# One routing of nine row tiles, late scatters and a second load queue in an attention and mixture-of-experts kernel

## The chip, the cores and the metric

The kernel runs on one core of a Trainium2 chip. The core has a matrix engine (PE, with PEld for its weight loads), a vector engine (DVE), an activation engine (ACT), a general engine (POOL, which also issues the indirect transfers) and a queue engine (SP, which issues most of the other transfers). The engines run their own instruction streams in order and wait for each other by semaphores. The metric is the device time of one execution in microseconds (us), the median of several runs.

## The reference

Three stages follow each other on 2304 tokens of width 512. The first is attention with 8 heads in which a row keeps only its 32 largest scores. The second routes each token to the one expert of eight with the largest gate logit. The third does the same with other weights, but only for tokens with a positive skip score, and adds its result to the token.

```python
kth = np.partition(scores, -32, axis=-1)[..., -32:-31]
attn = softmax(np.where(scores >= kth, scores, -1e9)) @ v
x = attn_out.transpose(0, 2, 1, 3).reshape(2304, 512)
e = argmax(x @ w_gate); g = softmax(x @ w_gate)[e]
x[mask_e] = g * (relu(x[mask_e] @ w1[e]) @ w2[e])                # layer one
x[mask_e] = x[mask_e] + g * (relu(x[mask_e] @ w1[e]) @ w2[e])    # layer two, tokens with x @ w_skip > 0
```

## The kernel before

**Attention.** The 4 batches are taken two at a time (a half), the 8 heads two at a time (a unit), so there are 8 units of 9 row tiles, 72 groups g in all. Units 0 to 3 are the first half, 4 to 7 the second. Each group passes through some twenty small stages, one letter each in `attention`: scores on PE (A), their copy to SBUF on ACT (AE), the search for the 32 largest on DVE (A1, lines 190 to 209), a check of the count with a sign pass on ACT and a product y on POOL (Bs, line 228) and its maximum on DVE (C, line 235), the masked exponentials (Dr, Dz, Dx, Dm), transposes and the product with v on PE (E, F), and the normalized row on DVE (Fin, line 346). For some (group, head) pairs POOL subtracts the mask (Dr, line 274); for the others DVE multiplies by it (Dm, line 291). The order is written out by hand: lines 389 to 421 give each stage of each group a step `tau` and a rank `z` within the step, and the instructions go out step by step. In the steady part a step does the work of one group for every stage, and the pattern of mask variants repeats every six groups.

**Routing.** When the last unit of a half has finished a row tile, the tile (x, three row tiles in one buffer, and parts, the shares of the gate logits) is routed: `Ga` adds seven small DVE instructions to the list `small`, `Gr` issues an exponential and small matrix products that count places, and adds eight more DVE instructions and the scatters. A1 takes one entry of `small` after each of its 14 MAX8 instructions; after step 73 the list is emptied at the end of each step. Before, `gate_tiles` routes three row tiles at a time (lines 637 to 676). In the first half the three sets are pulled apart by six steps each (line 402), and their nine scatters are spread over later steps by `LATE` (lines 410 and 411, `Sc`). A scatter (line 605) is an indirect transfer that POOL issues: 128 rows of 2056 bytes to their places in `ev.rows[0]` in HBM. The last three row tiles of the second half are routed one by one (`gate_rows`). The buffers x are five, so the third one of the second half takes the place of the first one of the first half.

**Weights.** `Moe.fetch(k)` loads chunk k (512 KB, eight chunks for each expert: four of w1, four of w2) on SP into one of eight raw buffers; `Moe.split(k)` makes a high part (ACT, line 765) and a low part (POOL or DVE, line 767) of it and then fetches the chunk that follows in the buffer. During attention three raw buffers exist; chunks 0 to 3 are split in steps 1, 2, 3 and 5, and chunks 4, 5 and 11 are loaded ahead.

**The layers.** `Moe.layer` loads the first expert's four blocks of rows (`load`, line 774, on SP), keeps PE warm with 26 transposes (line 691), loads the counts, and fetches chunks 6 to 10. `Moe.expert` transposes the blocks (`xT`, line 802), then runs eight first products (`mm1`, line 818) with the splits between them, and the second products (`mm2`, line 842). Blocks 2 and 3 of an expert stand under a condition on the count of its rows. `Moe.open` zeroes a part of XT on ACT (line 732).

Of the kernel before, what the change touches and what calls it, by code (L numbers as in the profile page):

```python
# [42 lines left out]
LATE = ((2, 4, 6), (2, 5, 8), (2, 5, 8))  # L43
# [67 lines left out]
def spare_places(tc, ev, s):  # L111


    ev.counts = s[:, 0, 0, 288:342].rearrange("p (a b) -> p a b", b=9)
    ev.onehot = [s[:, 0, 1, 288 + 54 * i:342 + 54 * i].rearrange("p (a b) -> p a b", b=9) for i in range(2)]
    ev.gates = [[s[:, 1, h, 288 + 48 * i + 24 * w:312 + 48 * i + 24 * w].rearrange("p (t e) -> p t e", e=8)
                 for h in range(2) for w in range(2)] + [s[:, 0, 0, 344 + 8 * i:352 + 8 * i]] for i in range(2)]
    ev.logits = [s[:, 1, 0, 384 + 8 * i:392 + 8 * i] for i in range(3)]
    ev.placed = [s[:, 1, 1, 384 + 8 * i:392 + 8 * i] for i in range(3)]
    tc.nc.vector.tensor_copy(ev.counts, ev.iosel[:, None, :].to_broadcast([128, 6, 9]))  # L120
# [23 lines left out]
def attention(tc, ev, q, k, v, during):  # L144
    nc = tc.nc
# [188 lines left out]
    def Fin(g):  # L334
        u, j = divmod(g, 9)
        e = G[g]
        kb, i, n = where[g]
        bp, hp = divmod(u, HP)
        if hp == 0 and j % 3 == 0:
            x[bp, j // 3] = ev.xp.tile([128, 3, HP * 128 + 2], F32, name="x", bufs=5)  # L340
            parts[bp, j // 3] = ev.xp.tile([128, 3, HP * 2, 8], F32, name="parts", bufs=5)
            nc.gpsimd.tensor_copy(x[bp, j // 3][:, :, HP * 128 + 1], ev.tok[:, bp * 9 + j:bp * 9 + j + 3])
        rows, shares = x[bp, j // 3][:, j % 3], parts[bp, j // 3][:, j % 3]
        for out, at, w in ((rows[:, hp * 128:hp * 128 + 128].rearrange("p (a b) -> p a b", a=2), 0, 64),
                           (shares[:, hp * 2:hp * 2 + 2], 128, 8)):
            nc.vector.tensor_tensor(out, e["po"][:, at:at + 2 * w].rearrange("p (a b) -> p a b", a=2),  # L346
                                    BT[kb]["ri"][:, 2 * i:2 * i + 2, None].to_broadcast([128, 2, w]), op=OP.mult)
        del G[g]

    def gated(g):  # L350

        u, j = divmod(g, 9)
        bp, hp = divmod(u, HP)
        n = 1 if g >= NG - 3 else 3 if j % 3 == 2 else 0
        return (bp, j // 3, j % 3 + 1 - n, n) if hp == HP - 1 and n else None

    def Ga(g):
        at = gated(g)
        if at:
            bp, k, t, n = at  # L360
            rt = bp * 9 + k * 3 + t
            if n > 1:
                a, rest, c = gate_tiles(tc, ev, sb, x[bp, k], parts[bp, k], rt, ev.gates[k % 2])
# [26 lines left out]
    for g in range(NG):  # L390
# [3 lines left out]
        for z, (nm, fn, at) in enumerate((  # L394
# [242 lines left out]
def gate_tiles(tc, ev, sb, x, parts, rt, places):  # L637

    nc = tc.nc
    v, n = nc.vector, x.shape[1]  # L640
    Dm = x.shape[2] - 2
    lg, order, row, mine, sums = places
    f = sb.tile([128, 3, 8], F32, name="tf", bufs=2)
    ed = sb.tile([128, 3, 8], F32, name="ted", bufs=2)
    ob = ev.onehots[rt // 3 % 2]
    ix = sb.tile([128, 3], I32, name="tix", bufs=2)
# [3 lines left out]
    def rest():  # L650
        nc.scalar.activation(ed, ed, AF.Exp)
        p = ev.ps.tile([128, 4, 8], F32, name="m", bufs=ev.mb)
        nc.tensor.matmul(p[:, :n + 1], ev.tri, ob[:, :n + 1], start=True, stop=False)
# [4 lines left out]
    def logits():  # L658
        v.tensor_reduce(out=lg, in_=parts.rearrange("p t h e -> p t e h"), op=OP.add, axis=AX.X)

    return [logits,
# [48 lines left out]
class Moe:  # L710
# [4 lines left out]
    def __init__(self, tc, ev, pool, weights):  # L715
        self.tc, self.ev, self.ws = tc, ev, weights
        self.W1 = [pool.tile([128, 2, 1024], F32R, name="w1_%d" % i) for i in range(4)]
        self.RAW = [pool.tile([128, 1024], F32, name="raw%d" % i) for i in range(3)]

    def open(self, sb, psum, posts):  # L720
# [10 lines left out]
        for c in range(4):  # L731
            self.tc.nc.scalar.activation(self.XT[:, c, :, 256:], self.ev.zrow[:, :512].rearrange("p (a n) -> p a n", a=2),
                                         AF.Copy)
        self.W1 += [sb.tile([128, 2, 1024], F32R, name="w1_%d" % (4 + i)) for i in range(NW - 4)]
        self.RAW += [sb.tile([128, 1024], F32, name="raw%d" % (3 + i)) for i in range(NR - 3)]
# [5 lines left out]
    def raw(self, k):  # L741

        return self.RAW[k % 3 if k < 4 else (k - 3) % NR]

    def fetch(self, k):
# [5 lines left out]
        raw, c = self.raw(k), k % 8  # L751
        if c < 4:
            self.tc.nc.sync.dma_start(raw, w1[e, c * 128:(c + 1) * 128, :])
        else:
            self.tc.nc.sync.dma_start(raw.rearrange("p (a d) -> p a d", a=2),
                                      w2[e, (c - 4) * 256:(c - 3) * 256, :].rearrange("(a p) d -> p a d", p=128))

    def split(self, k, vector=()):
# [9 lines left out]
        self.fetch(k + (3 if k < 3 else NR))  # L768

    def load(self, g, j):  # L770
# [3 lines left out]
        self.tc.nc.sync.dma_start(self.XG[g % 2][j], rows[r0:r0 + 128])  # L774
# [79 lines left out]
    def expert(self, g):  # L854
# [6 lines left out]
        self.optional(g, lambda j: self.xT(g, j))  # L861
        if e:
# [3 lines left out]
        if nxt:  # L866
            for j in range(BLOCKS[layer]):
                self.load(g + 1, j)
        k = 8 * g + 8
        for f in range(8):  # L870
# [4 lines left out]
            if f in FN:  # L875
                self.split(k, post.lo)
                k += 1
            self.tick()
            if f == 4 and nxt:
                self.counts(e + 1)  # L880
        if g == 15:
            self.tc.nc.gpsimd.drain()  # L882
        steps = {}
# [21 lines left out]
    def layer(self, layer, ns):  # L905
# [3 lines left out]
        for j in range(BLOCKS[layer]):  # L909
            self.load(g0, j)  # L910
# [5 lines left out]
        if layer == 0:  # L916
            for k in range(6, 3 + NR):
                self.fetch(k)
# [157 lines left out]
def attention_moe_kernel(ctx: ExitStack, tc, q, k, v, wg1, w11, w12, wskip, wg2, w21, w22, out):  # L1076
# [30 lines left out]
    ev.onehots = [consts.tile([128, 4, 8], BF, name="oh%d" % i) for i in range(2)]  # L1107
# [98 lines left out]
```

## Time and profile before

| | before |
|---|---|
| median of 3 runs | 1040.43 us (1039.23 to 1041.92) |
| the profiled execution, device time | 1037.0 us |
| its span in the trace | 1035.2 us |
| busy in the span: PE, DVE, ACT, POOL | 891.0, 747.0, 675.5, 627.7 us |

Attention fills roughly the first 493 us of the span, layer one the time up to about 800 us, layer two the rest. Busy shares over the whole span are therefore means over stages that have different limits. A row of a timeline gives start, duration, engine, line, operation, the tile written and the tiles read, and in brackets how long the engine had stood idle and what released it. DVE instructions are pipelined, so a printed duration reaches some 0.06 to 0.1 us into the next one; where work is priced below, starts are compared with starts where that can be done.

### The profile page before, as it was taken

The page shows a single profiled execution, that of the slowest core. Times are in us where ns is not written, and L with a number is a line of the kernel's source. Part 1 is how long each engine was busy: PE and PEld are TensorE (multiplying, and loading weights), DVE is VectorE, ACT ScalarE, POOL GpSimd, SP SyncE. Part 2 cuts the span into 40 slices and gives each one's busy share as a digit, 9 for nine tenths or more (in the row PEclk, how much of TensorE's full clock was granted, in tenths as well). Part 3 has the DMA queues.
Part 4 walks back from the last instruction along what each step waited for, and adds up shares of the span by engine and source line. Part 5 has one row for each costly group of instructions (what it writes and reads, how often), then busy time and mean ns, then how long its engine had stood idle before and what let it go on. Part 6 is the DMA issues. An engine that isn't in the chain of part 4 may idle for free. (4 is left out here: it accounts for less than half of the span.)

```text
span 1035.2 us, 20565 instructions
## 1 busy us (share of the span) xinstructions
PE 891.0 (86%) x6305; PEld 708.6 (68%) x6305; DVE 747.0 (72%) x3438; ACT 675.5 (65%) x1344; POOL 627.7 (61%) x446
## 2 busy tenths in 40 slices
PE   7578778877878778777899989998999899999997
PEld 5355545555555555555788879877887888888886
DVE  6999999999999999998328545356553356654362
ACT  6699999999989988975436434445553355543352
POOL 5888887887877978953225334344533366654454
PEclk9699999999989989989799999999999799999999
DMA  7897010100202000001635544466534367664540
GB/s 261 263 306 225 20 47 24 47 25 1 80 21 80 12 11 21 12 1 73 235 112 171 181 136 149 135 197 205 183 93 140 124 205 218 219 209 156 183 128 27
DMA packets 55032, 127.71 MB, mean 123 GB/s; under 512 B 8105, under 2 KB 8105, under 8 KB 54864
## 3 DMA queue, kind: packets, MB, share of 16 engines
q1 hardware_dynamic: 48464, 112.89, 34.8%
q0 software_dynamic: 6400, 12.65, 3.3%
q8 instruction: 97, 1.59, 0.6%
q14 instruction: 71, 0.58, 0.2%
HBM read 96.04 MB, written 37.86 MB: 129 GB/s over the span
## 5 line engine op out<-in xcount | busy, mean ns | idle before, releaser
L767 POOL TENSOR_TENSOR w<-raw,w 128x1024 fp32r<-128x1024 f32 x74 | 178.8, 2429 | 202.2 <-ACT w L765 151.9
L228 POOL TENSOR_TENSOR y<-s,sg 128x576 f32<-128x576 f32 x144 | 209.1, 1473 | 48.0 <-ACT sg L225 42.6
L842 PE MATMUL y<-w,h 128*128 128x512 f32 x936 | 227.8, 395 | 7.3 <-DVEq L791 3.3
L818 PE MATMUL hp<-xT,w 128*128 128x192 f32 (+4 forms) x1536 | 218.6, 300 | 5.3 <-DVE h L833 3.0
L818 PEld LDWEIGHTS hp<-xT,w 128*128 128x128 f32 x1536 | 208.5, 194 | 9.8 <-DVE h L833 5.6
L842 PEld LDWEIGHTS y<-w,h 128*128 128x128 f32 x936 | 171.4, 188 | 48.8 <-issue 8.4
L197 DVE MAX8 ca<-s 128x8 f32<-128x82 f32 (+1 forms) x1008 | 156.3, 228 | 6.2 <-ACT s L186 6.2
L274 POOL TENSOR_TENSOR r<-s,r 128x576 f32<-128x576 f32 x96 | 135.9, 1429 | 17.1 <-DVE r L270 11.9
L833 DVE SCALAR_TENSOR_TENSOR h<-hp,h 128x512 fp32r<-128x512 f32 (+1 forms) x128 | 77.9, 620 | 82.7 <-ACT h L832 82.6
L832 ACT ACTIVATE h<-hp 128x512 fp32r<-128x512 f32 (+1 forms) x128 | 69.8, 545 | 101.5 <-PE hp L818 94.2
L765 ACT ACTIVATE w<-raw 128x1024 fp32r<-128x1024 f32 x128 | 133.4, 1054 | 0.5 <-ACTq L791 0.5
L310 PE MATMUL m<-ident,p 128*128 128x128 f32 x576 | 96.5, 296 | 33.5 <-DVE parts L346 20.9
L225 ACT ACTIVATE sg<-s,tm 128x576 f32<-128x576 f32 x144 | 111.9, 796 | 7.1 <-POOL tm L216 6.8
L310 PEld LDWEIGHTS m<-ident,p 128*128 128x128 f32 x576 | 66.5, 148 | 72.3 <-ACT p L282 20.7
L767 DVE TENSOR_TENSOR w<-raw,w 128x1024 fp32r<-128x1024 f32 x54 | 94.7, 1753 | 21.5 <-ACTq L791 12.8
L99 PE MATMUL s<-kT,qT 64*128 64x288 f32 x512 | 86.3, 457 | 21.2 <-DVE kths L241 7.6
L235 DVE MAX8 my<-y 128x8 f32<-128x576 f32 x144 | 101.9, 746 | 1.6 <-POOL y L228 1.5
L186 ACT ACTIVATE s<-s 128x1152 f32<-128x1152 f32 (+1 forms) x73 | 81.6, 1119 | 20.5 <-PE s L99 10.6
L138 PE MATMUL m<-pT,v 128*64 128x128 f32 (+1 forms) x1280 | 90.2, 289 | 2.7 <-ACT pT L316 2.6
L316 ACT ACTIVATE pT<-m 128x512 f32<-128x512 f32 x144 | 80.9, 608 | 8.4 <-PE m L310 8.2
L138 PEld LDWEIGHTS m<-pT,v 128*64 128x64 f32 x1280 | 71.4, 151 | 15.4 <-ACT pT L316 5.0
L282 ACT ACTIVATE p<-r,neg 128x576 f32<-128x576 f32 x96 | 75.3, 785 | 6.4 <-POOL r L274 5.9
(160 smaller groups left out, 1225.6 us busy)
## 6 DMA issues: line engine op xcount, KB each, us to landing
raw<-in_moe_w_dram SPq DMA_DIRECT2D x128, 512.0 KB, 4.3
x<-zrow SPq DMA_DIRECT2D x16, 1028.0 KB, 19.0
xg<-x SPq DMA_DIRECT2D x56, 257.0 KB, 3.6
v<-in_v_dram SPq DMA_DIRECT2D x8, 576.0 KB, 3.7
kT<-in_k_dram SPq DMA_DIRECT2D x7, 576.0 KB, 3.8
qT<-in_q_dram SPq DMA_DIRECT2D x7, 576.0 KB, 4.9
out_dram<-yo,ix POOLq DMA_INDIRECT x40, 4.9
kT<-in_k_dram SPq DMA_DIRECT2D x2, 288.0 KB, 3.8
```

The costliest lines, as they stand in the source:

```text
L99: nc.tensor.matmul(p[:, c, :288], d["qT"][h, b, t * 128:t * 128 + 128], d["kT"][h, b, cs], start=True, stop=True)
L138: nc.tensor.matmul(po[i * 64:i * 64 + 64, cs], d["vt"][:, b, i, c] if c < 4 else d["v8"][i * 64:i * 64 + 64, b], pts[i][:, c, cs] if c < 4 ...
L197: nc.vector.max(out=ca[:, c], in_=e["s"][hh][:, cut[c]:cut[c + 1]])
L225: nc.scalar.activation(sg, e["s"][hh], AF.Sign, bias=bt["tm"][:, w:w + 1], scale=-ONE_BELOW, accum_out=bt["ac"][:, w:w + 1])
L228: nc.gpsimd.tensor_mul(y, e["s"][hh], sg)
L235: nc.vector.max(out=bt["my"][:, 2 * i + hh, 8:], in_=e["y"][hh])
L274: nc.gpsimd.tensor_tensor(r, e["s"][hh], r, op=OP.subtract)
L310: nc.tensor.transpose(pp[:, c], e["p"][:, hh, c * 128:c * 128 + 128], ident)
L765: nc.scalar.activation(t[:, 0], raw, AF.Copy)
L767: eng.tensor_tensor(t[:, 1], raw, t[:, 0].bitcast(F32), op=OP.subtract)
L818: nc.tensor.matmul(p[:, :W], self.w1(g, c)[:, a, fs], x[:, c, b, :W], start=(i == 0), stop=(i == 11))
L842: nc.tensor.matmul(p, self.HT[f][:, a, js], self.W2[f // 2][:, b, f % 2 * 512:f % 2 * 512 + 512], start=(f + a + b == 0), stop=(f == 7 and ...
```

## The change

- The first half's nine row tiles are routed in one set (`gate_tiles` with nine tiles, own tiles `whole`, `ev.half`, a ten-wide one-hot tile) after group 35, in steps 47 and 48; `Gr` follows `Ga` after one step instead of two, for the second half's first set too.
- Its nine scatters go out three each in steps 75, 76 and 77; the reciprocals are kept in a tile w, and one POOL copy for each three tiles puts them into the rows before the scatters.
- There are six x buffers. Two of them serve as raw buffers 1 and 2 in the first steps, and only one raw buffer is left of its own. Of the later chunks only chunk 4 is loaded during attention.
- In layer one, blocks 1 and 3 of the first expert are loaded on ACT's queue, and the zeroing of XT stands after these loads. Chunks 5 to 11 and the four blocks of the second expert are loaded on ACT's queue too: three right after the transposes of the first expert, and one in each of its eight first-product steps.

```diff
-LATE = ((2, 4, 6), (2, 5, 8), (2, 5, 8))
+LATE = (27, 27, 27, 28, 28, 28, 29, 29, 29)
+XB = 6
...
-            x[bp, j // 3] = ev.xp.tile([128, 3, HP * 128 + 2], F32, name="x", bufs=5)
+            x[bp, j // 3] = ev.xp.tile([128, 3, HP * 128 + 2], F32, name="x", bufs=XB)
...
-        n = 1 if g >= NG - 3 else 3 if j % 3 == 2 else 0
+        n = 1 if g >= NG - 3 else 9 * (j == 8) if bp == 0 else 3 * (j % 3 == 2)
...
-                ("Dx", Dx, m - 1), ("F", F, m + 2), ("Ga", Ga, m + 4), ("Gr", Gr, m + 6))):
+                ("Dx", Dx, m - 1), ("F", F, m + 2), ("Ga", Ga, m + 4), ("Gr", Gr, m + 5))):
...
-            if nm[0] == "G" and gated(g) and g < NG // 2:
-                at += g % 9 // 3 * 6
...
-                for t in range(3):
-                    plan.setdefault(at + LATE[g % 9 // 3][t], []).append((z, g, Sc))
+                for t in LATE:
+                    plan.setdefault(at + t, []).append((z, g, Sc))
...
-def gate_tiles(tc, ev, sb, x, parts, rt, places):
+def gate_tiles(tc, ev, sb, xs, parts, ob, places):
...
+    def send(t):
+        if n > 3 and t % 3 == 0:
+            nc.gpsimd.tensor_copy(xs[t // 3][:, :, Dm], w[:, t:t + 3])
+        scatter(tc, ev, ev.rows[0], ix[:, t:t + 1], xs[t // 3][:, t % 3], ev.group)
...
-            lambda: v.reciprocal(x[:, :, Dm], sums[:, n:2 * n]),
-            lambda: v.tensor_copy(ix[:, :n], sums[:, :n])] + [
-            lambda t=t: scatter(tc, ev, ev.rows[0], ix[:, t:t + 1], x[:, t], ev.group) for t in range(n)]
+            lambda: v.reciprocal(xs[0][:, :, Dm] if n == 3 else w, sums[:, n:2 * n]),
+            lambda: v.tensor_copy(ix, sums[:, :n])] + [lambda t=t: send(t) for t in range(n)]
...
-        return self.RAW[k % 3 if k < 4 else (k - 3) % NR]
+        return self.RAW[k % 3 if k < 4 else (k - 4) % NR]
...
-        self.fetch(k + (3 if k < 3 else NR))
+        if k < 1 or k > 2:
+            self.fetch(k + (1 if k == 3 else NR if k else 3))
...
+        first = []
+        if g == 0:
+            first = [lambda k=k: self.fetch(k, self.tc.nc.scalar) for k in range(5, 4 + NR)]
+            first += [lambda j=j: self.load(1, j, self.tc.nc.scalar) for j in range(BLOCKS[0])]
+            for i in range(3):
+                first.pop(0)()
...
-        if nxt:
+        if nxt and g:
             for j in range(BLOCKS[layer]):
                 self.load(g + 1, j)
...
+            if first:
+                first.pop(0)()
             self.tick()
...
         for j in range(BLOCKS[layer]):
-            self.load(g0, j)
+            self.load(g0, j, nc.scalar if layer == 0 and j % 2 else nc.sync)
+        if layer == 0:
+            for c in range(4):
+                nc.scalar.activation(self.XT[:, c, :, 256:], ...)
...
-        if layer == 0:
-            for k in range(6, 3 + NR):
-                self.fetch(k)
...
+        rows = [sb.tile([128, 3, Dm + 2], F32, name="x", bufs=XB) for i in range(2)]
+        moe.RAW += [t.rearrange("p t d -> p (t d)")[:, :1024] for t in rows]
```

## Rows read from the trace of the kernel before

**Rows 1.** Page: busy tenths of PE in 40 slices.
```profile
PE   7578778877878778777899989998999899999997
```
**Rows 2.** Stretches: start:end and length, DVE busy (instructions), clock, DMA share, GB/s.
```profile
195.47:208.49 13.02, 12.95 (x79) 1.00 0.26 93
195.47:231.95 36.48, 36.27 (x221) 1.00 0.15 51
231.95:270.00 38.05, 37.84 (x237) 0.91 0.10 33
270.00:312.23 42.23, 42.02 (x228) 0.92 0.10 34
312.23:350.17 37.94, 37.73 (x229) 0.91 0.16 55
350.17:390.15 39.98, 39.77 (x236) 0.91 0.04 15
390.15:428.85 38.70, 38.49 (x221) 0.91 0.04 15
428.85:443.90 15.05, 14.98 (x79) 1.00 0.05 19
```
**Rows 3.** Timeline of DVE, last steps of attention: line 291, POOL idle, first and last.
```profile
468.21 0.80 DVE L291 SCALAR_TENSOR_TENSOR p<-s,kths,e 128x576 f32<-128x576 f32 x1
...
477.04 0.81 DVE L291 SCALAR_TENSOR_TENSOR p<-s,kths,e 128x576 f32<-128x576 f32 x1
```
**Rows 4.** Timelines of POOL and then DVE around a scatter of the first half.
```profile
271.15 1.22 POOL L605 DMA_INDIRECT x<-x,tix  x1 [0.17 <-issue]
272.62 1.42 POOL L274 TENSOR_TENSOR r<-s,r 128x576 f32<-128x576 f32 x1
...
272.66 2.00 DVE L291 SCALAR_TENSOR_TENSOR p<-s,kths,e 128x576 f32<-128x576 f32 x1
```
**Rows 5.** Tile parts: the routing's first reduction, ns min/median/max, of three tiles and one.
```profile
L659 DVE TENSOR_REDUCE s<-parts x5: 486/494/517, 242.0 to 480.0; 128x24 f32<-128x192 f32 x5
L542 DVE TENSOR_REDUCE s<-parts x3: 274/276/276, 482.7 to 488.4; 128x8 f32<-128x64 f32 x3
```
**Rows 6.** Timelines of POOL and then DVE at the end of attention.
```profile
464.01 3.48 POOL L228 TENSOR_TENSOR y<-s,sg 128x576 f32<-128x576 f32 x2 [1.18 <-ACT sg L225]
480.30 1.04 POOL L605 DMA_INDIRECT x<-x,tix  x1 [12.80 <-DVE tix L675]
...
485.58 0.97 POOL L605 DMA_INDIRECT x<-x,tix  x1 [1.69 <-DVE tix L675]
...
491.97 0.97 POOL L605 DMA_INDIRECT x<-x,gix  x1 [0.30 <-DVE tcf L701]
...
491.11 0.15 DVE L633 CAST gix<-gf 128x1 int32<-128x1 f32 x1
```
**Rows 7.** Timelines in layer one: scatters of POOL, then DVE products that overlap them.
```profile
562.09 0.99 POOL L605 DMA_INDIRECT x<-yo,ix  x1 [0.63 <-DVE yo L1048]
...
600.79 1.79 POOL L605 DMA_INDIRECT x<-yo,ix  x1 [0.16 <-issue]
...
562.32 1.22 DVE L767 TENSOR_TENSOR w<-raw,w 128x1024 fp32r<-128x1024 f32 x1
...
600.32 1.40 DVE L767 TENSOR_TENSOR w<-raw,w 128x1024 fp32r<-128x1024 f32 x1 [0.26 <-ACTq L791]
```
**Rows 8.** Timeline of PE at the start of layer one.
```profile
501.92 1.94 PE L802 MATMUL m<-ident,xg 128*128 128x128 f32 x8 [1.70 <-DMA xg<-x]
504.61 7.68 PE L818 MATMUL hp<-xT,w 128*128 128x416 f32 x27 [0.75 <-ACT xT L804]
```
**Rows 9.** ACT's copies of chunks 5 and 9; then the raw tile's landing times, 490 to 530.
```profile
512.25 1.05 ACT L765 ACTIVATE w<-raw 128x1024 fp32r<-128x1024 f32 x1
...
525.93 1.05 ACT L765 ACTIVATE w<-raw 128x1024 fp32r<-128x1024 f32 x1
...
DMA to landing us min/median/max: 3.7/4.7/8.5
```

More of the change, by code (lines that the diff above doesn't have):

```diff
@@ L119, in spare_places @@
     ev.placed = [s[:, 1, 1, 384 + 8 * i:392 + 8 * i] for i in range(3)]
+    ev.half = [s[:, i, h, 408:480].rearrange("p (t e) -> p t e", e=8) for i in range(2) for h in range(2)] + [
+        s[:, 0, 0, 480:498]]
     tc.nc.vector.tensor_copy(ev.counts, ev.iosel[:, None, :].to_broadcast([128, 6, 9]))
@@ L339, in Fin @@
         if hp == 0 and j % 3 == 0:
-            x[bp, j // 3] = ev.xp.tile([128, 3, HP * 128 + 2], F32, name="x", bufs=5)
-            parts[bp, j // 3] = ev.xp.tile([128, 3, HP * 2, 8], F32, name="parts", bufs=5)
+            x[bp, j // 3] = ev.xp.tile([128, 3, HP * 128 + 2], F32, name="x", bufs=XB)
+            if bp == 0 and j == 0:
+                whole = ev.xp.tile([128, 9, HP * 2, 8], F32, name="whole", bufs=1)
+                parts.update({(0, i): whole[:, 3 * i:3 * i + 3] for i in range(3)}, whole=whole)
+            elif bp:
+                parts[bp, j // 3] = ev.xp.tile([128, 3, HP * 2, 8], F32, name="parts", bufs=3)
             nc.gpsimd.tensor_copy(x[bp, j // 3][:, :, HP * 128 + 1], ev.tok[:, bp * 9 + j:bp * 9 + j + 3])
@@ L361, in Ga @@
             rt = bp * 9 + k * 3 + t
-            if n > 1:
-                a, rest, c = gate_tiles(tc, ev, sb, x[bp, k], parts[bp, k], rt, ev.gates[k % 2])
+            if n == 9:
+                a, rest, c = gate_tiles(tc, ev, sb, [x[0, i] for i in range(3)], parts["whole"], ev.onehots[2], ev.half)
+            elif n > 1:
+                a, rest, c = gate_tiles(tc, ev, sb, [x[bp, k]], parts[bp, k], ev.onehots[k % 2], ev.gates[k % 2])
             else:
@@ L651, in rest @@
         nc.scalar.activation(ed, ed, AF.Exp)
-        p = ev.ps.tile([128, 4, 8], F32, name="m", bufs=ev.mb)
-        nc.tensor.matmul(p[:, :n + 1], ev.tri, ob[:, :n + 1], start=True, stop=False)
+        p = ev.ps.tile([128, n + 1, 8], F32, name="m", bufs=ev.mb)
+        nc.tensor.matmul(p, ev.tri, ob, start=True, stop=False)
         for k in range(n, 0, -1):
@@ L717, in __init__ @@
         self.W1 = [pool.tile([128, 2, 1024], F32R, name="w1_%d" % i) for i in range(4)]
-        self.RAW = [pool.tile([128, 1024], F32, name="raw%d" % i) for i in range(3)]
+        self.RAW = [pool.tile([128, 1024], F32, name="raw%d" % i) for i in range(1)]
     def open(self, sb, psum, posts):
@@ L730, in open @@
             self.tc.nc.vector.memset(p, 0.0)
-        for c in range(4):
-            self.tc.nc.scalar.activation(self.XT[:, c, :, 256:], self.ev.zrow[:, :512].rearrange("p (a n) -> p a n", a=2),
-                                         AF.Copy)
         self.W1 += [sb.tile([128, 2, 1024], F32R, name="w1_%d" % (4 + i)) for i in range(NW - 4)]
-        self.RAW += [sb.tile([128, 1024], F32, name="raw%d" % (3 + i)) for i in range(NR - 3)]
+        self.RAW[1:] = [sb.tile([128, 1024], F32, name="raw%d" % i) for i in range(1, NR)]
     def w1(self, g, c):
@@ L751, in fetch @@
         raw, c = self.raw(k), k % 8
+        queue = queue or self.tc.nc.sync
         if c < 4:
-            self.tc.nc.sync.dma_start(raw, w1[e, c * 128:(c + 1) * 128, :])
+            queue.dma_start(raw, w1[e, c * 128:(c + 1) * 128, :])
         else:
-            self.tc.nc.sync.dma_start(raw.rearrange("p (a d) -> p a d", a=2),
-                                      w2[e, (c - 4) * 256:(c - 3) * 256, :].rearrange("(a p) d -> p a d", p=128))
+            queue.dma_start(raw.rearrange("p (a d) -> p a d", a=2),
+                            w2[e, (c - 4) * 256:(c - 3) * 256, :].rearrange("(a p) d -> p a d", p=128))
     def split(self, k, vector=()):
@@ L773, in load @@
         r0 = e * (rows.shape[0] // 8) + j * 128
-        self.tc.nc.sync.dma_start(self.XG[g % 2][j], rows[r0:r0 + 128])
+        (queue or self.tc.nc.sync).dma_start(self.XG[g % 2][j], rows[r0:r0 + 128])
     def counts(self, e):
@@ L882, in expert @@
             self.tc.nc.gpsimd.drain()
+        while first:
+            first.pop(0)()
         steps = {}
@@ L1106, in attention_moe_kernel @@
     ev.wrong = consts.tile([128, 3], F32, name="wrong")
-    ev.onehots = [consts.tile([128, 4, 8], BF, name="oh%d" % i) for i in range(2)]
+    ev.onehots = [consts.tile([128, n, 8], BF, name="oh%d" % i) for i, n in enumerate((4, 4, 10))]
     for t in ev.onehots:
```

22 lines of the change are left out of this document (10 added, 12 removed).

## The prediction

> **What bounds the kernel now.** I read the page's slices first, for the stages. PE reaches nine tenths in slice after slice only from about slice 20, where the layers begin [rows 1]; attention, the first 493 us, has another limit. The stretches of attention, cut at every sixth pass of the top-32 search, show it: DVE is busy 36.27 of 36.48 us, and so in each of the others [rows 2]. So attention takes what DVE takes, and a microsecond that DVE gains or loses before about 468 us moves everything behind it. The layers are bound by PE, so an earlier start of layer one moves the end by as much.
>
> The stretches must then be compared with each other. The first half's rhythm is 36.48 us for six steps. In the second half, where the first half's rows are routed and scattered, five such stretches take 38.05, 42.23, 37.94, 39.98 and 38.70 us, in sum 196.90 where five undisturbed ones would take 182.40: 14.50 lost. The two steps after that take 15.05 where the same two steps of the rhythm take 13.02: 2.03 more [rows 2]. Thus 16.5 us are lost, and DVE is still busy all the time: it is given more to do, or the same work lasts longer.
>
> Both, as the rows show. The first of the five holds one set's routing and no scatter; it is 1.57 us long over the rhythm. Three sets make 4.7. The other 11.8 us come with the scatters. With POOL idle, the masked product of line 291 takes 0.81 us [rows 3]. Near a scatter POOL is later by the 1.22 us of the scatter, so that its subtraction of line 274 begins just before DVE's product instead of ending before it, and the product takes 2.00 us: it stands until POOL is done [rows 4]. A scatter costs DVE little by itself; it pushes POOL's long two-input products into DVE's.
>
> **The change part by part, against the profiled 1037.0 us** (the median of the runs shown is 3.4 above it; I carry the difference over).
>
> *One set instead of three.* Removed: three times 1.57 us of DVE work. Added: one set of nine tiles. Its first reduction goes from 192 to 576 columns; from 64 to 192 columns it grew by 0.218 us, 1.70 ns a column [rows 5], so 384 more columns cost 0.65. Ten further instructions go from 24 to 72 columns; at the same slope 0.08 each, at most 0.8, and nothing if the fixed part hides them. I take 0.45. The nine-tile set costs 1.57 + 1.1 = 2.7 (bounds 2.2 to 3.0). Gain 4.7 - 2.7 = 2.0. The matrix products for the places become ten instead of twelve and PE has room there. Gr one step after Ga puts them directly before the next group's scores, which share a PSUM tile with the routing and wait for it anyway; the results are read by DVE a pass later, so I charge no wait.
>
> *No scatter between steps 45 and 71.* The 11.8 us vanish if POOL falls back into the first half's pattern. What still differs from that half is the merged set in steps 47 and 48 and three token copies of POOL (line 342), which stood in the first half too. The first of the five stretches says that DVE work alone starts no collision: it cost 1.57, what its instructions cost. I charge 0.4 for a collision that is left; the bounds are 0 and the rival below. Gain 11.4.
>
> *The scatters in steps 75 to 77.* They queue on POOL behind the last products y, which end at 464.01 + 3.48 = 467.5. POOL is then idle for 12.80 us until the second half's first scatter at 480.30 [rows 6]. A scatter takes 0.97 and 0.30 to the next one, so nine take 11.4, and three copies with their gaps perhaps 1.5: the idle time is just filled. Who waits behind: the second half's scatters. A delay of up to 1.4 us is absorbed before the scatter at 485.58, which had 1.69 idle; beyond that it reaches the end nearly one to one, since the last index is ready at 491.26 and its scatter starts at 491.97 [rows 6]. Between 468.21 and 477.04 DVE runs eight of its two-input products [rows 3]. How such a product and a scatter meet, layer one shows twice: a scatter that begins during a product lasts 1.79 instead of 0.97, ending 0.86 after the product's end (601.72, 602.58), while a product that begins during a scatter takes 1.22 us, less than the 1.40 of the other [rows 7]. So DVE loses nothing and POOL waits: at most 8 x 0.75 = 6.0, that is 4.6 beyond the absorbed 1.4; if six in ten of nine scatters meet half a product, 9 x 0.6 x 0.4 = 2.2, that is 0.8. I take a loss of 0.8 (bounds 0 and 4.6).
>
> The page "SBUF — State Buffer" of the Trainium skill, section "Who interferes with whom", says that DVE and POOL share one port pair which whoever comes first holds for its whole instruction. By that rule a scatter would also hold up DVE's products; the rows at 562 us do not agree for a scatter, those at 272 us agree for a POOL product. What it would make of the sum is a rival.
>
> *Six buffers.* The second half's third x buffer no longer waits for scatters; DVE showed no idle time there, so nothing is gained, but without it steps 75 to 77 would be too late. Two of the buffers hold raw chunks only until step 3, nobody waits for them.
>
> *Layer one's loads.* PE stands 1.70 us for the conditional blocks of rows before 501.92 [rows 8]. On two queues they are issued two by two, and chunks 6 to 10 no longer follow at their heels. I take 1.0 (0 to 1.7) off. The zeroing of XT moves behind two issues on ACT, under the loads' flight, at no cost; were it uncovered, four activations of half the columns of a 1.05 us copy [rows 9] would cost about 2 us. Then chunks 5, 6 and 7, till now requested before the transposes, are requested on ACT near the start of the first product, at 504.61 less 1.0 [rows 8]. With the stretch's median landing of 4.7 us chunk 5 is there at 508.3 and with the longest, 8.5, at 512.1; it is wanted at 512.25 - 1.0 = 511.3 [rows 9]. The cover is 3 us at the median, and three PSUM tiles let PE run ahead of ACT: no cost. One issue then stands on ACT in each product step; I take each as shorter than the copy beside it. Uncovered, eight would cost up to 8 us; I charge none, as PE and not ACT ends the steps in these slices [rows 1].
>
> **Sum:** -2.0 - 11.4 + 0.8 - 1.0 = -13.6. The profiled 1037.0 becomes 1023.4, the median 1040.4 becomes **1026.8 us**. Its own range, with the bounds above, is 1023 to 1031.
>
> **The rivals.**
> - *The collisions stay.* The merged set in two steps running delays DVE against POOL by 2.7 us, and the products still meet until the rhythm is found again. For: the rhythm is tight, POOL's subtraction began only 0.04 us before the product that then stood [rows 4]. Against: the first stretch of the second half. If half of the 11.8 stays, 1033; if all stays, 1038.5.
> - *The scatter holds DVE.* Then eight products of the last steps wait up to 0.75 us each, 6 us, all on the path as DVE is the bound there too: 1026.8 + 6 - 0.8 = 1032. It is the rule of the Trainium skill named above. Against: rows 7.
> - *Expert 0 starves, slower than before.* Chunks 5 to 11 now start late, on a second queue that shares the transfer engines with SP's chunks 12 to 15. If they come one at a time at the longest landing of 8.5 us, chunk 9 is there at 503.6 + 5 x 8.5 = 546 where its copy stood at 525.93 [rows 9], ACT and then PE stand 20 us, and the time is 1026.8 + 20 = 1047. It costs something from (525.9 - 503.6) / 5 = 4.5 us a chunk on, and makes the kernel slower from 7.2 on, when the delay passes 13.6. For: chunks 5 and 11 are no longer there beforehand, and SP's chunks share the way. Against: the landings are those of chunks in flight together, with a median of 4.7 [rows 9], so each must come faster than that behind the one before.
> - *The change does not do what it says.* Scatters and loads keep their moment because a buffer or a semaphore holds them: within the measurement of 1040. The hand-written order speaks against it.
>
> **How the numbers follow.** Forecast 0.67; collisions stay 0.15 (mostly half of them); the scatter holds DVE 0.11; starving 0.03; no effect 0.04. The likeliest gives 1026.8. The range 1022.5 to 1034 takes in the forecast's bounds, the second rival and the half of the first. Over 0.3% (3 us, about what a measurement of this kernel tells from no change) faster: 0.93; same 0.04; slower 0.03.
>
> **What the changed profile would show.** Six-step stretches of 36.5 us in the second half, with one near 39.2 that holds the set; line 291 at 0.81 us up to step 71; one reduction of 576 columns at about 1.15 us; nine scatters on POOL without a gap of more than a product of DVE, the last one of all within 2 us of where the idle time put it; ACT's copies in expert 0 without waits for chunks. The prediction is wrong if line 291 is still stretched to 1.7 us and more before step 72, if DVE's products stretch beside scatters, or if PE stands in expert 0.

## The result and the profile after

| | before | after |
|---|---|---|
| median, runs side by side | 1040.08 us (1039.23 to 1042.05) | 1030.64 us (1027.86 to 1033.53) |
| ratio after / before | | 0.9898 (95% interval 0.9874 to 0.9923) |
| the profiled execution, device time | 1037.0 us | 1027.86 us |
| its span | 1035.2 us | 1026.0 us |

The change is faster by 1.0 per cent; two later groups of runs, on two chips, gave 0.986 and 0.985 (below). Lines of the changed kernel stand a little lower: 291 is now 294, 605 is 612, 346 is 353, 659 is 668, 765 is 769, 818 is 823.

The stretches of attention after, cut as those of [rows 2] (start:end and length, DVE busy, clock, DMA share, GB/s):

```profile
230.48:266.98 36.50, 36.29 (x221) 0.95 0.10 34
266.98:306.26 39.28, 39.07 (x237) 0.96 0.05 16
306.26:342.88 36.62, 36.41 (x221) 0.95 0.15 50
342.88:379.38 36.50, 36.29 (x221) 0.96 0.01 2
379.38:415.87 36.49, 36.28 (x222) 1.00 0.01 1
415.87:428.91 13.04, 12.97 (x80) 1.00 0.01 2
428.91:437.42 8.51, 8.51 (x37) 0.81 0.00 0
```

Four of the five long stretches are back at the first half's 36.5 (36.49 to 36.62); the one of 39.28 holds the nine-tile set. The five sum to 185.39 where [rows 2] sum to 196.90, and the two steps after them take 13.04 for 15.05: 13.52 us are gone.

What follows gives most of it back. The stretches are cut where the last round of a search pass starts (the MAX8 that writes my). From the last round of the last pass, here called the last search (437.42; before, 451.21), to the start of the last scatter went 491.97 - 451.21 = 40.76 us before, and 488.25 - 437.42 = 50.83 now. The timelines of POOL, DVE, PE and ACT after show where:

```profile
454.68 1.19 POOL L612 DMA_INDIRECT x<-x,tix  x1 [0.30 <-POOL x L665]
...
462.10 1.55 POOL L612 DMA_INDIRECT x<-x,tix  x1 [0.30 <-issue]
...
466.70 0.98 POOL L612 DMA_INDIRECT x<-x,tix  x1 [0.30 <-issue]
...
477.28 0.97 POOL L612 DMA_INDIRECT x<-x,tix  x1 [5.62 <-DVE tix L682]
...
486.97 0.97 POOL L612 DMA_INDIRECT x<-x,gix  x1 [4.87 <-DVE gix L640]
488.25 0.98 POOL L612 DMA_INDIRECT x<-x,gix  x1 [0.30 <-DVE tcf L707]
...
461.27 0.81 DVE L294 SCALAR_TENSOR_TENSOR p<-s,kths,e 128x576 f32<-128x576 f32 x1
465.11 0.29 DVE L353 TENSOR_TENSOR x<-m,ri 128x128 f32<-128x128 f32 x1 [2.29 <-PE m L335]
471.38 0.29 DVE L353 TENSOR_TENSOR x<-m,ri 128x128 f32<-128x128 f32 x1 [3.12 <-PE m L313]
484.34 0.29 DVE L353 TENSOR_TENSOR x<-m,ri 128x128 f32<-128x128 f32 x1 [4.64 <-PE m L593]
...
461.41 0.19 PE L658 MATMUL m<-oh,tri 128*128 128x32 bf16 x1 [1.77 <-DVE tf L673]
...
478.15 0.33 PE L141 MATMUL m<-p,v 64*64 64x64 f32 x4
...
483.13 0.28 ACT L330 ACTIVATE oT<-m 128x128 f32<-128x128 f32 x1 [5.73 <-remote]
```

The nine scatters go out without a gap and are done at 467.7; POOL then waits 5.62 and 4.87 us for indices of DVE, so POOL's queue is not what is late. DVE waits, 2.29, 3.12 and 4.64 us, each time for a row of PE. Two causes are seen. PE stood 1.77 us for the one-hot tile ahead of a group's transposes, because the places of the second half's first set are now asked for one step earlier. And the products of group 71 begin by 478.15, but ACT, which reads their result, gets it only at 483.13 (its row's `remote` means that the profile ties no instruction to the release): by the record of semaphores PE's update came 4.56 us after the modelled end of the product, and at 469.92 another had come 1.35 us late.

PE's first product of layer one (timeline of PE after; [rows 8] hold that of before):

```profile
498.49 0.46 PE L823 MATMUL hp<-xT,w 128*128 128x416 f32 x1 [0.75 <-ACT xT L809]
```

From the last scatter to the first product went 504.61 - 491.97 = 12.64 us before, 10.24 now. The whole account of the span, 9.2 us shorter: attention had started 1.44 earlier in this execution; 12.35 were won up to the last search (the 13.52 less 1.2 for a collision that is left in the last step); 10.07 lost up to the last scatter; 2.40 won up to the first product; 3.1 from there to the end (530.6 to 527.5), where nine later traces with the change's loads have 529.3 to 531.5, so these 3.1 are not the change's.

### The profile page after: what moved, and what is told of

It reads as the page before. It is cut to its first block, busy times and chain, and to the rows that moved or that the text cites. A ratio compares the mean times of both kernels' runs of the same rounds, so it can differ in the third digit from the quotient of the medians.

```text
span 1026.0 us, 20530 instructions
## 1 busy us (share of the span) xinstructions
PE 882.8 (86%) x6303; PEld 699.4 (68%) x6303; DVE 730.3 (71%) x3409; ACT 674.1 (66%) x1342; POOL 628.5 (61%) x449
## 5 line engine op out<-in xcount | busy, mean ns | idle before, releaser
L771 POOL TENSOR_TENSOR w<-raw,w 128x1024 fp32r<-128x1024 f32 x72 | 175.4, 2447 | 197.0 <-ACT w L769 162.0
L231 POOL TENSOR_TENSOR y<-s,sg 128x576 f32<-128x576 f32 x144 | 206.3, 1453 | 52.4 <-ACT sg L228 29.3
L200 DVE MAX8 ca<-s 128x8 f32<-128x82 f32 (+1 forms) x1008 | 153.8, 227 | 4.7 <-ACT s L189 4.7
L277 POOL TENSOR_TENSOR r<-s,r 128x576 f32<-128x576 f32 x96 | 136.1, 1431 | 18.5 <-DVE r L273 12.4
L313 PEld LDWEIGHTS m<-ident,p 128*128 128x128 f32 x576 | 64.4, 146 | 77.5 <-ACT p L285 24.0
L771 DVE TENSOR_TENSOR w<-raw,w 128x1024 fp32r<-128x1024 f32 x54 | 92.4, 1712 | 21.5 <-ACTq L796 12.8
L141 PE MATMUL m<-pT,v 128*64 128x128 f32 (+1 forms) x1280 | 87.6, 283 | 2.7 <-ACT pT L319 2.4
L141 PEld LDWEIGHTS m<-pT,v 128*64 128x64 f32 x1280 | 68.9, 147 | 15.4 <-ACT pT L319 5.8
```

Of the source, the lines that this page charges most:

```text
L141: nc.tensor.matmul(po[i * 64:i * 64 + 64, cs], d["vt"][:, b, i, c] if c < 4 else d["v8"][i * 64:i * 64 + 64, b], pts[i][:, c, cs] if c < 4 ...
L200: nc.vector.max(out=ca[:, c], in_=e["s"][hh][:, cut[c]:cut[c + 1]])
L231: nc.gpsimd.tensor_mul(y, e["s"][hh], sg)
L277: nc.gpsimd.tensor_tensor(r, e["s"][hh], r, op=OP.subtract)
L313: nc.tensor.transpose(pp[:, c], e["p"][:, hh, c * 128:c * 128 + 128], ident)
L771: eng.tensor_tensor(t[:, 1], raw, t[:, 0].bitcast(F32), op=OP.subtract)
```

## The experiments

Runs that follow each other under one heading share a chip only where that is said; every ratio is against runs of the kernel before on the same chip. Medians: the kernel before had 1037.4 us beside e1 to e4, 1040.0 beside e5 to e8, 1037.6 beside e9 to e12. "Excess" is the sum of what the steps up to the last search are longer than the shortest step at the same place of the six-step pattern in the first half; in the kernel before it was 18.5 us, in the first trace after 6.1. It depends by some 0.5 us on the counterparts that are taken.

| run | median us | ratio, 95% interval |
|---|---|---|
| e1 changed kernel | 1023.75 | 0.9857 (0.9832 to 0.9882) |
| e2 late scatters, three sets | 1026.52 | 0.9891 (0.9873 to 0.9908) |
| e3 one set, early scatters | 1036.67 | 0.9987 (0.9969 to 1.0004) |
| e4 places a step later | 1020.90 | 0.9841 (0.9812 to 0.9870) |
| e5, e6, e7 | 1039.7, 1033.4, 1039.5 (one execution each) | |
| e8 one queue for the blocks | 1032.51 | 0.9935 (0.9910 to 0.9960) |
| e9 changed kernel | 1021.52 | 0.9847 (0.9816 to 0.9877) |
| e10 places a step later | 1021.28 | 0.9844 (0.9812 to 0.9876) |
| e11 chunks behind the blocks | 1022.74 | 0.9860 (0.9821 to 0.9899) |
| e12 no nine scatters, half of the rows missing later | 1008.15 (one execution, not compared) | |

**Which part brings the gain: e2 and e3 (the chip of e1).** e2 has the late scatters alone. Each set keeps its own early routing, and its places come two steps after the reductions, as before:

```diff
-LATE = (27, 27, 27, 28, 28, 28, 29, 29, 29)
+LATE = ((32, 32, 32), (24, 24, 24), (16, 16, 16))
...
-        n = 1 if g >= NG - 3 else 9 * (j == 8) if bp == 0 else 3 * (j % 3 == 2)
+        n = 1 if g >= NG - 3 else 3 * (j % 3 == 2)
...
-                ... ("Gr", Gr, m + 5))):
+                ... ("Gr", Gr, m + (6 if g < NG // 2 else 5)))):
...
+            if nm[0] == "G" and gated(g) and g < NG // 2:
+                at += g % 9 // 3 * 6
...
```

> The late scatters alone: three sets routed six steps apart as in the kernel before, all else as in the changed kernel. Theory (the scatters' occupation of POOL causes the collisions): line 294 stays at 0.80 to 0.81 us up to step 71, the stretches from step 45 to 71 sum to 182.4 + 4.7 = 187 us, against 185.2 of the changed kernel, so the time is 2 us above the changed kernel's at the last search and at most 2 above it at the end. Rival (it is the merging that keeps DVE and POOL in step): at least half of the 11.8 us of collisions is back, line 294 at 1.7 to 2.4 us in many steps, and the time is 6 us or more above the changed kernel at the last search.

Stretches of e2 as above. Then a wait of DVE in the stretch from 382.85, what ACT and PE did before it, the granted clock there (PE busy in the place of DVE), and last the same products of e1:

```profile
231.24:269.31 38.07, 37.86 (x237) 0.90 0.10 32
269.31:307.83 38.52, 37.85 (x228) 0.92 0.05 16
307.83:344.79 36.96, 36.75 (x230) 0.95 0.15 50
344.79:382.85 38.06, 37.85 (x237) 0.89 0.01 2
382.85:420.49 37.64, 36.37 (x222) 0.93 0.00 1
420.49:433.50 13.01, 12.94 (x79) 0.97 0.01 2
...
386.54 0.22 DVE L241 TENSOR_TENSOR s<-ac,s 128x54 f32<-128x54 f32 x1 [1.06 <-ACT s L189]
385.37 1.13 ACT L189 ACTIVATE s<-s 128x1152 f32<-128x1152 f32 x1 [1.79 <-issue]
383.05 2.21 PE L100 MATMUL s<-kT,qT 64*128 64x288 f32 x8
378.30:384.90 6.60, 6.60 (x55) 0.50 0.00 0
...
378.02 1.25 PE L100 MATMUL s<-kT,qT 64*128 64x288 f32 x8
```

No product of line 294 is stretched before step 71: the rival fell. The five sum to 189.25, 7.65 under the kernel before; with 2.04 in the two steps after them that is 9.69 us by moving the scatters alone. The merged set takes another 3.86 off (189.25 to 185.39). The time is 2.8 us above e1, its neighbour, with intervals that overlap.

Not all of the 3.86 is the sets'. Two stretches are 0.67 and 1.27 longer than DVE is busy, where the others are 0.21 longer: DVE waits 0.47 and 1.06 us for ACT's copy of a group's scores (line 189). ACT had stood idle 1.54 and 1.79 us before it; the bracket names no releaser, but each copy starts 0.11 us after PE's score products end. These took 2.30 and 2.21 us, all or most of it at a granted TensorE clock of 0.50 (1.2 GHz), where e1's took 1.25 at 1.00. The same wait, behind score products of 2.07 to 2.30 us at such a clock, stands in e3 (0.38), e6 (1.40 and 0.64) and e10 (0.79), all of which route one set. So these 1.5 us go with the clock of that execution, which was also the slowest of e2's four (1029.29 against a median of 1026.52). Without them the late scatters bring 11.2 and the merged set 2.3.

e3 changes only `LATE = (2, 4, 6, 7, 9, 12, 15, 18, 21)`.

> The merged set alone: its nine scatters go out in steps 50 to 69, most of them where the kernel before had them; all else as in the changed kernel. Theory (scatters cause the collisions): line 294 at 1.7 to 2.4 us near the scatters, 8 to 12 us more than the changed kernel up to the last search. At the end less of it is left, since the last steps of the changed kernel lost some 8 to 10 us that a later DVE would not lose: 3 to 8 us above the changed kernel, 1033 to 1038. Rival (merging keeps the step): line 294 at 0.81, within 2 us of the changed kernel at the last search and at the end.

A stretch of e3 and a product in another:

```profile
389.00:429.70 40.70, 40.49 (x222) 0.91 0.04 14
...
391.66 5.03 DVE L294 SCALAR_TENSOR_TENSOR p<-s,kths,e 128x576 f32<-128x576 f32 x1
```

The collisions are back, and larger than expected: excess 22.7 (1.8 of it in steps 27 to 29, before any scatter), the last search 18.0 us behind e1's, the time 12.9 us above it, and no longer distinguishable from the kernel before. The theory held in direction; my 3 to 8 us were too few, because products stood 5.0 and 4.6 us and the last steps returned only 2.

**What it is about a scatter: e5, e6, e7 (one chip).** e5 keeps the scatters late and puts POOL's delay alone where e3 had them:

```diff
+    def five():
+        for i in range(5):
+            nc.gpsimd.tensor_copy(dl, ev.tok[:, :3])
...
+                for t in (2, 4, 6, 7, 9, 12, 15, 18, 21):
+                    plan.setdefault(at + t, []).append((z, g, Dl))
```

> The changed kernel with nine groups of five small POOL copies (128x3, about 0.2 us each, to a tile that nobody reads) where the run with early scatters had its scatters, steps 50 to 69; the real scatters stay in steps 75 to 77, so no transfer is added. It measures the disputed cost by itself: 1.0 to 1.3 us of POOL's time, without an indirect transfer. Theory (POOL's delay pushes its long two-input instructions into DVE's): line 294 at 1.7 us and more in several steps, 8 to 20 us more than the changed kernel at the last top-32 search. Rival (it is the transfer: its traffic, or what the scatter does beyond occupying POOL): line 294 at 0.81 up to step 70 and the last search within 2 us of the changed kernel's.

POOL, then DVE, near one of the nine groups:

```profile
348.00 1.41 POOL L395 COPY dl<-tok 128x3 f32<-128x3 f32 x5
...
349.57 1.41 POOL L277 TENSOR_TENSOR r<-s,r 128x576 f32<-128x576 f32 x1
350.93 3.31 POOL L231 TENSOR_TENSOR y<-s,sg 128x576 f32<-128x576 f32 x2
...
349.74 1.86 DVE L294 SCALAR_TENSOR_TENSOR p<-s,kths,e 128x576 f32<-128x576 f32 x1
```

No transfer, and the picture of [rows 4]: POOL's subtraction begins 0.17 us before the product, which stands. Excess 13.2, 8.0 more than e1's 5.2: the low end of what was expected. The rival as it stood (nothing without a transfer) fell. But e3's scatters, planned in the same steps, made 15.7 more than e1 besides the 1.8 ahead of any scatter, so the delay alone shows about half. Where e3 and e5 are furthest apart, in steps 63 and 69 with the steps behind them, e5 lost 1.6 and 2.0 and e3 4.2 and 3.7. What a scatter does there beyond delaying POOL stays open.

e6 and e7 send three of the nine scatters early, six steps apart: `LATE = (6, 12, 18, 28, 28, 28, 29, 29, 29)` and `(9, 15, 21, 28, ...)`.

> The changed kernel with three of the nine scatters early, each six steps apart, planned in steps 54, 60 and 66 (the places of the six-step pattern at which the kernel before and the run with early scatters lost least); the other six stay late. Theory (a scatter costs DVE only where POOL has no idle time to take it before its next long instruction): at most 0.3 us for each, the last search within 1 us of the changed kernel's. Rival (any early scatter sets off collisions): line 294 above 1.5 us after each, 1 to 4 us for each, 3 to 12 in sum.

> The same, but the three early scatters are planned in steps 57, 63 and 69, half a pattern later, where the kernel before lost most. Theory: line 294 at 1.7 us and more after each, 2 to 4 us for each, 6 to 12 us more than the changed kernel at the last search, though it is the same count of the same scatters as in the run with steps 54, 60 and 66. Rival (place does not matter): the same loss as that run within 1.5 us.

POOL and DVE at the first scatter of e6, then of e7:

```profile
331.93 1.20 POOL L612 DMA_INDIRECT x<-x,tix  x1 [2.54 <-issue]
...
333.38 2.77 POOL L277 TENSOR_TENSOR r<-s,r 128x576 f32<-128x576 f32 x2
336.11 2.75 POOL L231 TENSOR_TENSOR y<-s,sg 128x576 f32<-128x576 f32 x2
...
335.88 3.30 DVE L273 TENSOR_SCALAR r<-s,kths 128x576 f32<-128x576 f32 x1
```

```profile
345.78 1.20 POOL L612 DMA_INDIRECT x<-x,tix  x1 [0.30 <-POOL x L665]
347.02 0.27 POOL L219 TENSOR_SCALAR tm<-my 128x6 f32<-128x6 f32 x1
347.24 1.41 POOL L277 TENSOR_TENSOR r<-s,r 128x576 f32<-128x576 f32 x1
348.59 2.75 POOL L231 TENSOR_TENSOR y<-s,sg 128x576 f32<-128x576 f32 x2
...
346.79 5.18 DVE L294 SCALAR_TENSOR_TENSOR p<-s,kths,e 128x576 f32<-128x576 f32 x1
```

e7's three steps are 4.38, 3.76 and 3.74 us long over their counterparts: 11.9, the upper end of what the theory had. e6's scatters of steps 60 and 66 cost 0.00 and 0.01, but that of step 54 cost 2.84, ten times the bound, and up to the last search e6 lost 6.1 us more than e8 on the same chip, where its theory allowed 1. So place decides, but not the number of the step alone: in e6 DVE had already lost 1.5 us in step 45, ahead of any scatter, and what stood after 54 was another operation, line 273 (0.66 us where undisturbed). The loss in step 45 is the wait for ACT told of under e2: PE's score products took 2.30 us at a granted clock of 0.50, where e9's took 1.25 at 1.00.

What decides how long a product stands is not shown either. In step 63 of e7 and of e5 POOL's subtraction begins 0.20 and 0.17 us before the product, and line 231 follows it without a gap. In e7 the product takes 4.55 us and stands behind both products y; in e5 it takes 1.85, and the first product y lasts 1.93 instead of 1.41.

**Attention's last steps: e1, e4 (one chip), e9, e10, e12 (another).**

> The changed kernel itself, once more, for a second trace of attention's last steps. In the first trace the lead over the kernel before was 13.8 us at the last top-32 search and 3.7 us at the last scatter, and PE's copy for group 71 came 4.6 us late around 478 us. If that late stretch of PE belongs to the kernel (its code or its traffic at that place), it stands again at the same instructions, 4 to 5 us long, and the last scatter is near 488 us again. If it was one execution's chance, ACT's wait for it shrinks from 5.73 to about 1 us, the last scatter comes near 484, and the profiled time is some 4 us under the first one, 1023 to 1024. Both theories expect the waits of steps 74 to 78 (DVE for POOL's y, DVE for the copy behind the matrix products of the places) again.

> The changed kernel once more, as the neighbour of the three runs beside it. In two earlier groups of runs it stood at 0.990 and 0.986 of the kernel before. In its first trace, and in the four of the second group of experiments, PE's semaphores came 1.3 to 4.6 us late around the scatters of attention's last steps; in its second trace and its three neighbours none did. Theory (the late semaphores go with the early matrix products of the places): they appear here and not in the run with the later products. Rival (they go with the chip on which a group runs): either both runs show them or neither does.

e4 and e10 put the places of the second half's first set back to two steps after the reductions; e12 is e10 without the nine scatters (their three POOL copies stay):

```diff
-                ... ("Gr", Gr, m + 5))):
+                ... ("Gr", Gr, m + (5 if g < NG // 2 else 6)))):
```
```diff
+        if n == 3:
             scatter(tc, ev, ev.rows[0], ix[:, t:t + 1], xs[t // 3][:, t % 3], ev.group)
```

> As the changed kernel, but the second half's first set issues its matrix products for the places two steps after its first reductions, as before, not one. Theory (the early products hold PE: 1.77 us of waiting ahead of a group's transposes, then 2.29 us of DVE waiting for that group's rows in step 78): both waits are gone, the last scatter comes 2 us earlier, and the time is 1.5 to 2.5 us under the changed kernel's. Rival (the last steps are bound by ACT's and POOL's chain and by PE's late stretch anyway): DVE's wait moves to another instruction and the time is the changed kernel's within 1 us.

> The changed kernel with the second half's matrix products for the places two steps after the first reductions, as before, once more and in more rounds. Theory: DVE's waits in step 78 are gone as in the first trace of this kernel, and the time is 2 to 4 us under the changed kernel's, 0.2 to 0.4 per cent. Rival (that difference was the spread of single executions): the two agree within 1 us.

> The kernel of the run beside it with later products, without the nine scatters of the first half: half of the rows are missing in the layers, so only attention's last steps count, not the total time. It gives the price of nine scatters there. Prediction on record: 0.8 us, with bounds 0 and 4.6, all through POOL's queue. Theory after the first traces (POOL's chain is not the last to arrive there, and DVE's products take 0.81 us beside a scatter): the time from the last top-32 search to the last scatter is within 0.5 us of the neighbour's, some 41 us. Rival (scatters hold up DVE or PE): 2 us shorter or more, and PE's late semaphores, if the neighbour shows them, are gone.

From the last search to the last scatter:

| before | first trace after | e1 | e9 | e4 | e10 | e12 |
|---|---|---|---|---|---|---|
| 40.76 | 50.83 | 44.08 | 42.19 | 41.33 | 41.19 | 40.67 |

e11, with early places, took 42.16. DVE's waits for rows, POOL's wait for the second set and the last scatter, in e9 and then e10:

```profile
463.15 0.29 DVE L353 TENSOR_TENSOR x<-m,ri 128x128 f32<-128x128 f32 x1 [0.72 <-PE m L335]
...
469.80 0.29 DVE L353 TENSOR_TENSOR x<-m,ri 128x128 f32<-128x128 f32 x1 [0.79 <-PE m L335]
473.05 0.97 POOL L612 DMA_INDIRECT x<-x,tix  x1 [1.55 <-DVE tix L682]
...
479.43 0.97 POOL L612 DMA_INDIRECT x<-x,gix  x1 [0.30 <-DVE tcf L707]
```

```profile
465.09 0.29 DVE L353 TENSOR_TENSOR x<-m,ri 128x128 f32<-128x128 f32 x1 [0.38 <-PE m L335]
472.29 0.97 POOL L612 DMA_INDIRECT x<-x,tix  x1 [1.08 <-DVE tix L682]
...
478.67 0.98 POOL L612 DMA_INDIRECT x<-x,gix  x1 [0.30 <-DVE tcf L707]
```

The late semaphores of PE: 1.35 and 4.56 us in the first trace; on one chip 4.4 in e6, 3.0 in e7, 1.6 and 3.6 in e5, 2.4, 1.3 and 1.9 in e8; none in the eight traces of the two other groups, with either place of the products. The five traces that have them also record only 865 to 868 updates of PE's semaphore, where the others record 874 (e12, which leaves work out, 872). So e9's theory fell and its rival held: among versions of the changed kernel they go with the group of runs, which is a chip. That the change has no part in them is not shown: the one trace of the kernel before has none, and no version without the nine scatters or with later places ran where they occur. The same edit then costs 10.07 us in the last steps with them, and 1.4 to 3.3 without.

Placing the products later takes 1.0 (e9 to e10) or 2.8 us (e1 to e4) off this stretch. PE's wait for the one-hot tile, 1.5 to 1.8 us in all traces with early places, is gone in e4, e10 and e12, and of DVE's waits for rows in e9 (0.72 and 0.79) one of 0.38 is left. The larger figure holds more than the places: in e1 and in e2 (44.05) TensorE's granted clock is 0.50 for 3.4 us from 26 us after the last search, and in the first trace from 24; in e9, e11 and e3 (42.19, 42.16, 42.05) and in e4 and e10 it is 1.00 from 13 to 38 us after it. At that clock early places cost 0.7 to 1.0. Whether they bring on the fall of the clock is not shown. In the medians the later places are worth 2.9 us on one chip and 0.2 on the other, well inside the intervals; neither version can be told to be faster. The nine scatters cost 41.19 - 40.67 = 0.5 us, one trace against one: e12's theory held, at the edge of its 0.5.

**The start of layer one: e8 and e11 (two chips).** e8 loads the four blocks on SP (`nc.sync` in `layer`); e11 keeps two queues and requests chunks 5 to 11, and the second expert's blocks, on SP as before (the requests on ACT are gone; only the added lines are shown):

```diff
+        if layer == 0:
+            for k in range(5, 4 + NR):
+                self.fetch(k)
         for e in range(8):
             self.expert(g0 + e)
```

> The changed kernel with all four blocks of rows of the first expert loaded on SP, the chunks of weights still late on ACT's queue. In the kernel before the first product of layer one starts 12.64 us after the last scatter's start, in the two traces of the changed kernel 10.24 and 11.15. Theory (two queues bring the blocks earlier): 1 us of that is lost again, some 11.7 from last scatter to first product, and the time is 1 us longer. Rival (what helped is that no chunks follow at the blocks' heels): 10.2 to 11.2 as in the changed kernel, and no difference in time.

> The changed kernel with the chunks 5 to 11 requested on SP right behind the first expert's blocks and the second expert's blocks on SP too, as the kernel before had it; the first blocks stay on two queues. Theory (both the second queue and the chunks out of the way bring the first product earlier): from the last scatter to the first product 11.6 to 12.0 us, where the changed kernel takes 10.2 to 11.2, the run with one queue 11.7 and the kernel before 12.6; the time 0.5 to 1 us longer. Rival (the queue alone): 10.8 us, the same time. A third reading (late chunks starve the first expert a little): the first product later but the end earlier than the changed kernel's.

The last scatter and the first product, of e8 and then of e11:

```profile
486.17 0.97 POOL L612 DMA_INDIRECT x<-x,gix  x1 [0.30 <-DVE tcf L706]
...
497.87 2.48 PE L823 MATMUL hp<-xT,w 128*128 128x416 f32 x5 [0.75 <-ACT xT L809]
```

```profile
477.81 0.97 POOL L612 DMA_INDIRECT x<-x,gix  x1 [0.30 <-DVE tcf L707]
...
488.85 11.41 PE L823 MATMUL hp<-xT,w 128*128 128x416 f32 x47 [0.75 <-ACT xT L809]
```

11.70 with one queue, 11.04 with two and the chunks behind the blocks, 10.24 to 11.21 (median 10.85) in ten traces with the change's loads, 12.64 before. One queue costs 0.8, in one trace and outside that spread: as expected. The chunks behind the blocks cost 0.2 against that median, inside the spread of the ten, so the rival of e11 held and its theory fell. From the first product to the end they take 529.4 and 530.7, within the 529.3 to 531.5 of the change: late chunks starve nobody and bring nothing. e8's time is not compared, since its chip had PE's late semaphores and no run of the changed kernel beside it.

## Why the prediction came out as it did

- **DVE sets attention's time; 13.4 us go up to the last search.** Right: 13.52 by the stretches, and 12.35 (first trace) or 13.2 (e1, e9) up to the last search. The split was right too, as far as e2 tells: its three sets cost 6.85 (189.25 - 182.40), of which 1.5 are the waits at a clock of 0.50, so 5.3 where I had 4.7. Merging then brought 2.3 where I had 2.0, and the scatters 11.2 where I had 11.4. By e2's trace as it stands it would be 3.9 and 9.7; one trace does not tell how often such waits occur.
- **The nine-tile set costs 2.7.** Right: 39.28 - 36.5 = 2.8. Its 576-column reduction takes 1.19 us (I had 1.15), its other instructions 0.22 instead of 0.17.
- **A collision left, 0.4.** In step 71 products of 1.69 and 1.95 (first trace) or one of 2.05 (e1, e9) remain; e11 has none above 0.82. The step takes 8.5 or 7.7 us where before it took 7.3: 1.2 in the first trace, so too low there, and 0.4 in e1 and e9. By the sign that the prediction set (1.7 us and more before step 72) this one step counts against it.
- **Nine scatters fill POOL's idle time, 0.8.** Right: 0.5 by e12. They took 13.0 us from the first one's start and POOL waited for DVE after them. But in the first trace the last scatter came 10.07 us later behind the last search than before (3.3 in e1, 1.4 in e9), where the prediction gave it 2, by the next two points.
- **"I charge no wait" for the places one step earlier.** This is the step that failed. For the second half's first set PE stands 1.77 us for them ahead of a group's transposes, and DVE waits for that group's rows: 0.7 to 1.0 us of this stretch at a clock of 1.00, up to 2.8 with the clock's fall. I had argued from the first half, where a pass of the search lies between; after step 73 the small list is emptied at once, and there is no such pass.
- **The late semaphores of PE** were in no row of before and not foreseen; they are up to some 6 of the 10.07 us of the first trace (1.35 and 4.56); the rest beyond the places is not taken apart. They may also be why this measurement came out 3.8 us above the forecast and those of the two later groups below it (by their ratios the 1040.4 becomes 1025.6 and 1024.5); that is argued from the traces, not shown in the unprofiled executions.
- **Loads on two queues, 1.0.** Under-sized: 1.8 by the median (12.64 to 10.85), just over the upper bound of 1.7. No cost of late chunks: right.
- **The rivals.** The collisions did not stay. The scatter does not hold DVE: the eight products between 454 and 468 us, most of them beside scatters, take 0.80 to 0.81, and it is the scatter that lasts up to 1.55. Nobody starves. The rival that came nearest in time, 1032 for a scatter that holds DVE, came near by chance: DVE did lose time in the last steps, but waiting for PE.
- **The range.** The bounds of the parts, without the rivals, add up to 1024.4 to 1031.9, not to 1023 to 1031; the measured 1030.64 lies in both. It lies there although the places and the semaphores of PE were not in the sum: attention's end cost more than forecast, layer one's start less.

By the rule of the Trainium skill (page "SBUF — State Buffer", section "Who interferes with whom") whoever comes first holds the shared ports for its whole instruction. For one POOL product the rows agree: in e5 DVE's product, 0.17 us behind POOL's subtraction, took 1.86 us. In e7 they do not: by its printed start the product came first, at 346.79, yet it ended at 351.97, behind four instructions of POOL of which the first began at 347.02 and the last ended at 351.34. The same section counts `tensor_scalar` among the operations that can use both port pairs; the 3.30 us of line 273 in e6, where it takes 0.66 undisturbed, agree.

## What to carry to other kernels

A small instruction on an engine with little idle time costs its neighbours what it delays, not what it lasts: look at what runs back to back behind it and whom that meets, and move it to a place where the engine waits anyway. When a gain has two causes that share a stretch, undo one of them before you price either, and look at the granted clock of that trace before you put a wait down to the edit. A step moved earlier for one group of work is moved for all that the same line schedules: price it at the end of the pipeline too, where the slack that hid it is gone.

## What the hardware showed that was not expected

- A waiting DVE instruction may fail to get in between POOL instructions that follow each other without a gap: 5.03 us (e3), 5.18, 4.55 and 4.54 us (e7) for a product of 0.81. In e5 it did get in, after 1.86 us. What decides is open.
- In attention, PE at a granted clock of 0.50 can hold up DVE by way of ACT: score products of 2.07 to 2.30 us instead of 1.25 (e2, e3, e6, e10), a late copy by ACT, and 0.38 to 1.40 us of waiting, though DVE is the engine that sets the time.
- PE's semaphores can come 1.3 to 4.6 us after the modelled end of their matrix products, in attention's last steps while scatters run: in the first trace and all four of one chip, and in none of eight traces on two others (the first trace's chip is not on record). The kernel before showed none in its one trace. What holds them up stays open; no run separated the scatters' transfers from the rest on such a chip.
